# Two batches of attention products in float32, and the second layer's weight splits spread out

## The chip, the cores and the metric

The kernel runs on one core of a Trainium2 chip. The core has TensorE (PE, matrix products; PEld is its weight load), VectorE (DVE), ScalarE (ACT), GpSimd (POOL) and SyncE (SP, which only issues transfers here). The metric is the device time of one execution in microseconds (us), the median of the runs shown.

## The reference

Three steps follow each other on float32 activations and float64 weights. Shapes: 8 batches, 8 heads, 576 positions, head size 64, 32 memory slots.

```python
a = softmax over positions of phi                # per batch and head, 576 x 32
k_m, v_m = a^T k, a^T v                          # 32 x 64 each
attn = softmax(q k_m^T / 8) ; out = attn v_m     # 576 x 64
x = out as (4608, 512)
x = (silu(x @ w_gate) * (x @ w_val)) @ w_out     # 512 -> 1536 -> 512
h = x @ w_in ; g = h if h > 0 else exp(h) - 1    # 512 -> 2048
x = g @ w_out2                                   # 2048 -> 512
```

q and k are drawn 20 times as wide as the other inputs, so the scores are sharp and the products that lead to them must be close to float32.

## The kernel before, in words

**Number format.** TensorE takes float32 here in a reduced form (F32R in the code). To keep the precision, an operand is cut in two: `hi` is a copy to F32R by ACT, `lo` is the rest, subtracted by DVE or POOL. A product is then three matmuls: hi by hi, hi by lo, lo by hi. Weights come as float64 words and are cut by `split_w` (L76 to L90): ACT scales the high word (L82), DVE does four operations (L83, L84, L86, L87), ACT makes hi (L88), POOL makes lo in two operations (L89, L90). Two raw buffers (`wr`) and two pairs of work buffers (`wv`, `wc`) serve all 68 splits: 24 of `w1g` (gate and value weights), 12 of `w1o`, 32 of `w2` (16 units of the second layer with two halves each).

**Attention.** `front_tasks` of a batch transposes the softmax of phi (`a_T`), cuts five chunks of k and v (`kv_prep`), multiplies (`kv_mm`, L251), masks (`kv_out`) and transposes k_m and v_m (`k_T`, `v_T`). `back_tasks` cuts five chunks of q (`q_prep`), makes scores (`score`, L303), does the softmax over 32 slots and transposes the result into `at`. Chunk buffers come in twos, so chunk c+2 is loaded when chunk c has been cut.

**Phase 1.** For every batch, units 0 to 3 of the first layer in two halves of 288 positions: `gate1`, `val1` (its last DVE operation is `h`, L171, then `hh` by ACT and `hl` by DVE), `down1`. The attention tasks of the following batches are put between the units by `tick`. Batch 0's attention and part of batch 1's stand alone at the start.

**Phase 2.** Units 4 to 11 for every batch, 16 halves of 8 units. `vw2` and `fold` multiply attention values into the gate weights; from batch 4 on these are read back (`load_vw`, `vwl`). 16 splits of `w2` are asked for in batches 3 and 4, at every second unit; the other 16 are asked for behind the phase.

**Layer 2.** Nine blocks of 512 tokens, each 16 units: 12 matmuls up (`pu`), the ELU chain on DVE and ACT (`unit3`, L662 to L666, then `hh` and `hl`), 12 matmuls down, two units later (`LAG`).

A scheduler that builds a timeline of its own sets the order on each engine, starting from the order in which the code is written; `tc.issue_after(x)` forbids it to put what follows ahead of x. The engines then run their instructions strictly in that order.

Of the kernel before, what the change touches and what calls it, by code (L numbers as in the profile page):

```python
# [8 lines left out]
F32 = mybir.dt.float32  # L9
# [18 lines left out]
NCH = 5  # L28
NWA = 24
NWB = 22  # L30
NWD = 2
NWC = 18
NM = 4
# [3 lines left out]
def attention_moe_moe(ctx: ExitStack, tc: tile.TileContext, qT, phiT, kv, w1g, w1o, w2, out):  # L37
# [59 lines left out]
    def load_w(store, u, i, src, pool):  # L97
        raw = wr_p.tile([128, 512, 2], I32, tag="wr", name="wr")
        nc.sync.dma_start(out=raw, in_=src.rearrange("p (n t) -> p n t", t=2))
        hi = pool.tile([128, 512], F32R, tag="w", name="whi")  # L100
        lo = pool.tile([128, 512], F32R, tag="w", name="wlo")
        split_w(raw, hi, lo)
        store[u][i] = hi, lo
# [48 lines left out]

    last = {}

    def gate1(b, u, at, s0, silu):
# [11 lines left out]
    def val1(b, u, at, s0, s, silu):  # L167
        pv = ps_gv.tile([128, HS], F32, tag="g", name="pv")
        up1(pv, VW[b, u // 2], 256 * (u % 2) + 128, at, s0)
        h = t_p.tile([128, HS], F32, tag="h", name="h")  # L170
        stt(out=h, in0=s, scalar=1.0 if silu else 0.5, in1=pv, op0=ALU.mult, op1=ALU.mult)  # L171
        return split_h(h_p, h, HS)
# [19 lines left out]
    class Batch:  # L192
        def __init__(self, b):
            self.b = b
            self.kvr, self.kvs, self.qr, self.qs = {}, {}, {}, {}

        def load_phi(self):
            self.ph = fr_p.tile([128, 2, S], F32, tag="ph", name="ph")
            nc.sync.dma_start(out=self.ph, in_=phiT[self.b].rearrange("g p s -> p g s"))

        def load_kv(self, c):
            n = chunk(c)
            t = fr_p.tile([128, 2, 512], F32, tag="kvr", name="kvr", bufs=2)
            nc.sync.dma_start(out=t[:n], in_=kv[self.b, 128 * c:128 * c + n])
            self.kvr[c] = t

        def load_q(self, c):
            n = chunk(c)
            t = bk_p.tile([128, 512], F32, tag="qr", name="qr", bufs=2)
            nc.sync.dma_start(out=t[:, :4 * n], in_=qT[self.b, :, 512 * c:512 * c + 4 * n])  # L210
            self.qr[c] = t
# [387 lines left out]
    load_wf(*heads[0][:2])  # L599
    w2q = [(3, wb_p)] * 8 + [(4, wa_p)] * 8  # L600
    vwq = []
    ldq = {(2 * b - 1) * (NU1 - UA) + 2 * p - UA + 3: (b, p) for b in range(NM, B) for p in range(UA // 2, NU1 // 2)}
    for b in range(B):
        for hf in range(2):
# [4 lines left out]
            for u in range(UA, NU1):  # L609
# [44 lines left out]
    def unit3(u, xt):  # L654
# [77 lines left out]
```

## Time and profile before

| what | value |
|---|---|
| median of 3 runs (lowest, highest) | 1769.15 us (1768.7, 1770.59) |
| the profiled execution: its time, its span | 1770.36 us, 1768.6 us |
| granted TensorE clock, mean | 0.972 |
| busy share of the span: PE, DVE, ACT, POOL | 94%, 63%, 43%, 16% |
| chain that ended last: PE, DVE, DMA | 74%, 14%, 6% |

The time is 1.8 us more than the span, which runs from the first to the last instruction. A share over the whole span says little here: the four stages (start, phase 1, phase 2, layer 2) differ. The rows by stretch further down are the ones to read.

### The profile page before, as it was taken

The numbers are of one execution on the slowest core, as the hardware profiler recorded it, in microseconds if no ns is written. First come the engines' busy times: TensorE is split into PE (matmuls) and PEld (weight loads), VectorE is DVE, ScalarE is ACT, GpSimd is POOL, SyncE is SP. The second block draws the span as 40 slices with busy tenths as digits, with TensorE's granted clock in tenths as the row PEclk, the third lists the DMA queues.
The fourth block names the chain that finished last, engine by engine and source line by source line (L and its number), as shares of the span: only waits on it lengthen the run. The fifth ranks groups of instructions, "written<-read, shape, count | busy, mean of one in ns | idle before, by whom it ended". The sixth has DMA issues, their size and how long they took to land.

```text
span 1768.6 us, 24239 instructions
## 1 busy us (share of the span) xinstructions
PE 1667.3 (94%) x9296; PEld 1468.6 (83%) x9296; DVE 1108.2 (63%) x1837; ACT 760.2 (43%) x1457; POOL 282.8 (16%) x199
## 2 busy tenths in 40 slices
PE   5589999989999998889999799999999999999998
PEld 3379989979899997889998678888888888888887
DVE  7988777697853358644448965555545555555554
ACT  5456655555533344423334534343434343434332
POOL 4632222253510024200004410000000000000000
PEclk7689999999999999999999899999999999999999
DMA  6455544235624346843333301010101010101000
GB/s 218 158 196 186 169 157 157 89 135 158 208 86 157 100 128 194 252 140 106 112 102 105 109 1 48 1 48 1 48 1 48 1 48 1 48 1 48 0 24 24
DMA packets 89396, 168.57 MB, mean 95 GB/s; under 512 B 16576, under 2 KB 48320, under 8 KB 87232
## 3 DMA queue, kind: packets, MB, share of 16 engines
q1 hardware_dynamic: 65216, 132.41, 23.1%
q10 hardware_dynamic: 24064, 34.62, 6.4%
q8 instruction: 73, 1.20, 0.3%
q14 instruction: 43, 0.35, 0.1%
HBM read 108.27 MB, written 50.33 MB: 90 GB/s over the span
## 4 chain that ended last, share of the span: by engine, by line
PE 74%; DVE 14%; DMA 6%; issue 3%; ACT 2%; ACTq 0%; POOL 0%; SPq 0%; DVEq 0%; POOLq 0%
PE acc L678 7%; PE acc L677 7%; PE acc L676 7%; PE pu L651 7%; PE pu L650 7%; PE pu L652 7%; PE acc L142 3%; PE acc L143 3%; PE acc L144 3%; DVE wv L84 2%; PE pv L137 2%; PE pg L137 2%; DVE wc L87 2%; PE pv L138 2%; PE pv L139 2%
## 5 line engine op out<-in xcount | busy, mean ns | idle before, releaser
L650 PE MATMUL pu<-x1s,whi 128*128 128x512 f32 x576 | 225.0, 391 | 9.4 <-DVE g L666 9.4
L678 PE MATMUL acc<-whi,hl 128*128 128x512 f32 x576 | 222.7, 390 | 2.5 <-DVE hl L150 2.5
L676 PE MATMUL acc<-whi,hh 128*128 128x512 f32 x576 | 224.3, 389 | 0.7 <-ACT hh L148 0.7
L651 PE MATMUL pu<-x1s,whi 128*128 128x512 f32 x576 | 224.7, 390 | 0.0
L652 PE MATMUL pu<-x1s,wlo 128*128 128x512 f32 x576 | 224.6, 390 | 0.0
L677 PE MATMUL acc<-wlo,hh 128*128 128x512 f32 x576 | 224.1, 389 | 0.0
L665 DVE SCALAR_TENSOR_TENSOR g<-e,g 128x512 f32<-128x512 f32 x144 | 101.7, 707 | 162.8 <-ACT g L664 162.8
L89 POOL TENSOR_TENSOR wv<-wv,whi 128x512 f32<-128x512 f32 x68 | 103.7, 1526 | 531.9 <-ACT whi L88 434.0
L663 ACT ACTIVATE e<-g 128x512 f32<-128x512 f32 x144 | 90.6, 630 | 213.2 <-DVE g L662 213.1
L148 ACT ACTIVATE hh<-g 128x512 fp32r<-128x512 f32 x144 | 90.9, 632 | 209.2 <-DVE g L666 207.7
L171 DVE SCALAR_TENSOR_TENSOR h<-s,pv 128x288 f32<-128x288 f32 x192 | 86.0, 448 | 132.7 <-PE pv L139 115.8
L150 DVE TENSOR_TENSOR hl<-g,hh 128x512 fp32r<-128x512 f32 x144 | 100.5, 698 | 92.1 <-ACT hh L148 92.1
L142 PE MATMUL acc<-hh,whi 128*128 128x288 f32 x512 | 148.9, 295 | 5.2 <-ACT hh L148 5.2
L143 PE MATMUL acc<-hh,wlo 128*128 128x288 f32 x512 | 149.5, 295 | 0.0
L144 PE MATMUL acc<-hl,whi 128*128 128x288 f32 x512 | 143.2, 297 | 5.4 <-DVE hl L150 5.4
L150 DVE TENSOR_TENSOR hl<-h,hh 128x288 fp32r<-128x288 f32 x192 | 109.0, 570 | 61.5 <-ACT hh L148 61.1
L148 ACT ACTIVATE hh<-h 128x288 fp32r<-128x288 f32 x192 | 84.5, 442 | 139.7 <-DVE h L171 128.3
L650 PEld LDWEIGHTS pu<-x1s,whi 128*128 128x128 f32 x576 | 108.4, 188 | 32.3 <-DVE g L666 9.8
L662 DVE TENSOR_SCALAR g<-pu 128x512 f32<-128x512 f32 x144 | 99.1, 689 | 55.0 <-PE pu L652 54.9
L678 PEld LDWEIGHTS acc<-whi,hl 128*128 128x128 f32 x576 | 108.0, 188 | 26.1 <-DVE hl L150 3.7
L676 PEld LDWEIGHTS acc<-whi,hh 128*128 128x128 f32 x576 | 108.2, 188 | 23.9 <-ACT hh L148 1.5
L651 PEld LDWEIGHTS pu<-x1s,whi 128*128 128x128 f32 x576 | 108.6, 189 | 22.5
(128 smaller groups left out, 4039.0 us busy)
## 6 DMA issues: line engine op xcount, KB each, us to landing
kvr<-kv SPq DMA_DIRECT2D x32, 512.0 KB, 4.2
wr<-w SPq DMA_DIRECT2D x32, 512.0 KB, 3.6
wr<-w1g SPq DMA_DIRECT2D x24, 512.0 KB, 3.8
atd<-at SPq DMA_DIRECT2D x8, 1152.0 KB, 4.7
p1d<-p ACTq DMA_DIRECT2D x64, 144.0 KB, 2.7
at<-atd SPq DMA_DIRECT2D x8, 1152.0 KB, 7.4
p1l<-p1d SPq DMA_DIRECT2D x16, 576.0 KB, 4.5
x1d<-p1l SPq DMA_DIRECT2D x16, 576.0 KB, 3.3
```

Of the source, the lines that this page charges most:

```text
L89: nc.gpsimd.tensor_tensor(out=v, in0=v, in1=hi.bitcast(F32), op=ALU.subtract)
L142: mm(ps, lhsT=w[0][:, ms], rhs=hs[0], start=start, stop=False)
L143: mm(ps, lhsT=w[1][:, ms], rhs=hs[0], start=False, stop=False)
L144: mm(ps, lhsT=w[0][:, ms], rhs=hs[1], start=False, stop=stop)
L148: act(out=hh, in_=h, func=AF.Copy)
L150: tt(out=hl, in0=h, in1=hh.bitcast(F32), op=ALU.subtract)
L650: mm(ps, lhsT=wh[:, k, :], rhs=xh, start=k == 0, stop=False)
L651: mm(ps, lhsT=wh[:, k, :], rhs=xl, start=False, stop=False)
L652: mm(ps, lhsT=wl[:, k, :], rhs=xh, start=False, stop=k == KD - 1)
L676: mm(accs[c], lhsT=hs[0][:, cs], rhs=wh, start=u == 0, stop=False)
L677: mm(accs[c], lhsT=hs[0][:, cs], rhs=wl_, start=False, stop=False)
L678: mm(accs[c], lhsT=hs[1][:, cs], rhs=wh, start=False, stop=u == NU2 - 1)
```

## The change

Batches 0 and 1 (`NF = 2`) keep k, v, q, the softmax of phi and k_m as float32 and multiply them in one float32 matmul instead of three: no `kv_prep`, no `q_prep`, no `al`, and the scores are one matmul of 64 columns and an ACT copy instead of two matmuls, an ACT copy and a DVE addition. All five chunks of a batch are loaded in one go; they take over the buffers in which hi and lo were. `split_w` now stands behind the last `h` (or, in layer 2, the last `g`) that was written before it. The splits of `w2` are asked for one at units 5 and 9 of every half from batch 3 on (20), and two per unit in the first six units of layer 2 (12).

```diff
-NWC = 18
+NWE = 8
+NWC = 10
+NF = 2
@@ load_w
-        split_w(raw, hi, lo)
+        with tc.issue_after(last["h"].ins) if "h" in last else nullcontext():
+            split_w(raw, hi, lo)
@@ val1, and the same for the last operation of unit3
-        stt(out=h, in0=s, scalar=1.0 if silu else 0.5, in1=pv, op0=ALU.mult, op1=ALU.mult)
+        last["h"] = stt(out=h, in0=s, scalar=1.0 if silu else 0.5, in1=pv, op0=ALU.mult, op1=ALU.mult)
@@ Batch
+            self.f32 = b < NF
+            self.kv_tag = [("kvr", "kvr", "kvh", "kvh", "kvl")[c - b] if self.f32 else "kvr" for c in range(NCH)]
...
-            tt(out=self.al[o], in0=ps[:n, :nch], in1=self.ah[o].bitcast(F32), op=ALU.subtract)
+            if not self.f32:
+                tt(out=self.al[o], in0=ps[:n, :nch], in1=self.ah[o].bitcast(F32), op=ALU.subtract)
@@ kv_prep and q_prep
+            if self.f32:
+                return
@@ kv_mm
+            if self.f32:
+                t = self.kvr.pop(c)
+                for g in range(2):
+                    mm(self.kvp[g], lhsT=self.ah[:n, c, 128 * g:128 * g + 128],
+                       rhs=t[:n, :, 256 * g:256 * g + 256], start=c == 0, stop=c == 4)
+                return
@@ score
+            if self.f32:
+                q = self.qr.pop(c)[:, :4 * n].rearrange("p (i s) -> p i s", i=4)
+                ps = ps_at.tile([128, 4, 64], F32, tag="at", name="ps_sc")
+                for i in range(4):
+                    mm(ps[:n, i, :], lhsT=q[:, i, :], rhs=self.kT[:, i // 2, i % 2, 0:64], start=True, stop=True)
+                act(out=self.sc[:n, c, :], in_=ps[:n].rearrange("p i n -> p (i n)"), func=AF.Copy)
+                return
@@ the start
-    Bs[0].load_kv(0)
-    Bs[0].load_kv(1)
-    Bs[0].load_q(0)
-    Bs[0].load_q(1)
+    for c in range(NCH):
+        Bs[0].load_kv(c)
+    for c in range(NCH):
+        Bs[0].load_q(c)
@@ phase 2
-    w2q = [(3, wb_p)] * 8 + [(4, wa_p)] * 8
+    w2q = [wb_p] * 8 + [wa_p] * 8
...
-                if u % 2 == 0 and w2q and w2q[0][0] <= b:
-                    more_w2(w2q.pop(0)[1])
+                if u % 4 == 1 and b >= NM - 1:
+                    more_w2(w2q.pop(0))
+        if b == NM - 1:
+            st_vq.close()
+            we_p = ctx.enter_context(tc.tile_pool(name="we", bufs=NWE))
+            w2q += [we_p] * 4
@@ between phase 2 and layer 2
-    more_w2(wb_p, 3)
-    more_w2(wa_p, 4)
     wc_p = ctx.enter_context(tc.tile_pool(name="wc", bufs=NWC, side="right"))
-    more_w2(wc_p, len(todo2))
+    w2q = [wb_p] * 3 + [wa_p] * 4 + [wc_p] * 5
@@ layer 2, behind each unit
+            for _ in range(2):
+                if w2q:
+                    more_w2(w2q.pop(0))
```

What the scheduler makes of it is seen in three places. The first is TensorE's queue at the start, batch 0's front. Before, with `kvh` and `kvl` the cut chunks and `al` the rest of the transposed softmax:

```order
L236 MATMUL ps_aT<-ident,ph 128x128 x4
L260 MATMUL ps_kvm<-kvh,ah 128x512 x2
L236 MATMUL ps_aT<-ident,ph 128x128 x4
L261 MATMUL ps_kvm<-kvh,al 128x512
L262 MATMUL ps_kvm<-kvl,ah 128x512
L261 MATMUL ps_kvm<-kvh,al 128x512
L262 MATMUL ps_kvm<-kvl,ah 128x512
```

With the change (L244 is the transposition, L269 the float32 product, L291 the transposition of k_m):

```order
L244 MATMUL ps_aT<-ident,ph 128x128 x4
L269 MATMUL ps_kvm<-kvr,ah 128x512 x2
L244 MATMUL ps_aT<-ident,ph 128x128 x4
L269 MATMUL ps_kvm<-kvr,ah 128x512 x2
L244 MATMUL ps_aT<-ident,ph 64x128 x2
L269 MATMUL ps_kvm<-kvr,ah 128x512 x6
L291 MATMUL ps_kT<-ident,kvm 128x128 x4
```

Ten products stand where thirty stood, and nothing in the row needs a cut operand.

The second is SP's queue at the start (`ph` is phi, `kvr` and `qr` the chunks, `wr` the raw weights). Before:

```order
L199 DMA ph<-phiT 128x2x576
L204 DMA kvr<-kv 128x1024 x2
L210 DMA qr<-qT 128x512 x2
L99 DMA wr<-w1g 128x1024 x2
L204 DMA kvr<-kv 128x1024 x2
L210 DMA qr<-qT 128x512 x2
L99 DMA wr<-w1g 128x1024
L199 DMA ph<-phiT 128x2x576
```

With the change:

```order
L206 DMA ph<-phiT 128x2x576
L211 DMA kvr<-kv 128x1024 x4
L211 DMA kvr<-kv 64x1024
L217 DMA qr<-qT 128x512 x4
L217 DMA qr<-qT 128x256
L211 DMA kvr<-kv 128x1024
L103 DMA wr<-w1g 128x1024 x2
L217 DMA qr<-qT 128x512
L211 DMA kvr<-kv 128x1024 x2
```

The first two raw weights stand behind twelve loads instead of five.

The third is DVE's queue in the first units of layer 2. Before, from the first two `g` on (L83, L84, L86, L87 are the splits):

```order
L662 TENSOR_SCALAR g<-pu 128x512 x2
L83 TENSOR_SCALAR wc<-wv 128x512
L84 SCALAR_TENSOR_TENSOR wv<-wv,wc 128x512
L665 SCALAR_TENSOR_TENSOR g<-e,g 128x512 x2
L86 TENSOR_SCALAR wc<-wv 128x512
L83 TENSOR_SCALAR wc<-wv 128x512
L666 TENSOR_TENSOR g<-g,pu 128x512 x2
L87 SCALAR_TENSOR_TENSOR wc<-wr,wc 128x512
L84 SCALAR_TENSOR_TENSOR wv<-wv,wc 128x512
L150 TENSOR_TENSOR hl<-g,hh 128x512 x2
L86 TENSOR_SCALAR wc<-wv 128x512
L662 TENSOR_SCALAR g<-pu 128x512 x2
```

With the change, a few units in (L87, L88, L90, L91 are the splits, L710, L713, L714 and L155 the four operations of a unit):

```order
L90 TENSOR_SCALAR wc<-wv 128x512
L87 TENSOR_SCALAR wc<-wv 128x512
L714 TENSOR_TENSOR g<-g,pu 128x512
L710 TENSOR_SCALAR g<-pu 128x512
L91 SCALAR_TENSOR_TENSOR wc<-wr,wc 128x512
L88 SCALAR_TENSOR_TENSOR wv<-wv,wc 128x512
L155 TENSOR_TENSOR hl<-g,hh 128x512
L90 TENSOR_SCALAR wc<-wv 128x512
L713 SCALAR_TENSOR_TENSOR g<-e,g 128x512
L710 TENSOR_SCALAR g<-pu 128x512
L91 SCALAR_TENSOR_TENSOR wc<-wr,wc 128x512
L714 TENSOR_TENSOR g<-g,pu 128x512
```

The units are the same; of the splits, 14 stand from the end of phase 2 on in the row before, and 12 in the row of the change, over the first twelve units. The 16 earlier ones, which stand between the 109th and the 132nd `h` before, have become 20 between the 114th and the 190th, of 192.

## Rows read from the trace of the kernel before

**Rows 1.** busy time by stretch: start:end, length, five engines, PEclk, DMA share, GB/s
```profile
0.00:100.00 100.00, 55.81 (x184) 38.71 (x184) 87.36 (x122) 47.80 (x85) 51.38 (x41) 0.69 0.59 193
100.00:200.00 100.00, 97.20 (x651) 88.73 (x652) 84.53 (x162) 63.46 (x139) 31.36 (x19) 1.00 0.54 181
360.00:500.00 140.00, 127.11 (x821) 118.47 (x820) 122.43 (x201) 69.89 (x151) 63.97 (x47) 0.95 0.52 165
500.00:640.00 140.00, 139.70 (x961) 133.91 (x960) 49.74 (x110) 46.40 (x101) 0.00 (x0) 1.00 0.38 117
640.00:660.00 20.00, 20.00 (x138) 19.15 (x138) 13.46 (x21) 9.46 (x19) 10.44 (x8) 1.00 0.35 111
640.00:780.00 140.00, 123.14 (x806) 115.75 (x806) 91.98 (x153) 59.55 (x126) 45.47 (x32) 0.96 0.61 191
780.00:940.00 160.00, 160.00 (x1210) 160.00 (x1209) 70.78 (x155) 56.59 (x128) 0.00 (x0) 1.00 0.33 102
940.00:1030.00 90.00, 74.12 (x369) 61.91 (x369) 83.26 (x114) 42.61 (x75) 45.89 (x32) 0.94 0.31 101
1200.00:1400.00 200.00, 200.00 (x884) 165.58 (x884) 107.67 (x160) 76.51 (x123) 0.00 (x0) 1.00 0.07 22
```

**Rows 2.** DVE groups from 0 to 110: count, busy us, mean ns, idle before
```profile
L87 DVE SCALAR_TENSOR_TENSOR wc<-wr,wc 128x512 f32<-128x512 uint32 x14 | 16.4, 1168 | 0.1
L84 DVE SCALAR_TENSOR_TENSOR wv<-wv,wc 128x512 int32<-128x512 int32 x14 | 12.4, 892 | 0.1
L190 DVE TENSOR_TENSOR kvl<-kvr,kvh 128x1024 fp32r<-128x1024 f32 x7 | 11.5, 1650 | 0.7 <-ACT kvh L247 0.6
L83 DVE TENSOR_SCALAR wc<-wv 128x512 int32<-128x512 int32 x14 | 9.1, 655 | 2.9 <-ACT wv L82 2.9
L86 DVE TENSOR_SCALAR wc<-wv 128x512 int32<-128x512 int32 x14 | 6.7, 483 | 0.0
...
L190 DVE TENSOR_TENSOR ql<-qr,qh 128x512 fp32r<-128x512 f32 x4 | 3.8, 954 | 0.0
L240 DVE TENSOR_TENSOR al<-ps_aT,ah 128x512 fp32r<-128x512 f32 x5 | 3.4, 678 | 0.0
L190 DVE TENSOR_TENSOR kvl<-kvr,kvh 64x1024 fp32r<-64x1024 f32 x2 | 3.3, 1648 | 0.1
...
L315 DVE TENSOR_TENSOR sc<-ps_sc,sct 128x256 f32<-128x256 f32 x6 | 2.5, 415 | 0.1
```

**Rows 3.** DVE in order of time (start, length): the fourth h
```profile
108.42 0.45 DVE L171 SCALAR_TENSOR_TENSOR h<-s,pv 128x288 f32<-128x288 f32 x1 [0.55 <-PE pv L139]
```

**Rows 4.** TensorE in order of time: start, length, instruction
```profile
14.36 0.63 PE L261 MATMUL ps_kvm<-kvh,al 128*128 128x512 f32 x1
14.79 0.63 PE L262 MATMUL ps_kvm<-kvl,ah 128*128 128x512 f32 x1
...
36.88 0.37 PE L312 MATMUL ps_sc<-kT,ql 128*128 128x64 f32 x1
37.06 0.46 PE L311 MATMUL ps_sc<-kT,qh 128*128 128x128 f32 x1
```

**Rows 5.** waits of the whole span: who, for whom, us in total, times, longest
```profile
ACT vwl L549 <- DMA vwl<-vwd: 22.3, 14, 4.9
...
PE pu L650 <- DVE g L666: 9.4, 1, 9.4
```

**Rows 6.** DVE groups from 940 to 1025, around the start of layer 2
```profile
L665 DVE SCALAR_TENSOR_TENSOR g<-e,g 128x512 f32<-128x512 f32 x8 | 7.6, 955 | 0.0
L150 DVE TENSOR_TENSOR hl<-g,hh 128x512 fp32r<-128x512 f32 x8 | 6.4, 816 | 0.2 <-ACT hh L148 0.2
L662 DVE TENSOR_SCALAR g<-pu 128x512 f32<-128x512 f32 x9 | 5.9, 678 | 0.0
L150 DVE TENSOR_TENSOR hl<-h,hh 128x288 fp32r<-128x288 f32 x6 | 5.9, 990 | 0.5 <-ACT hh L148 0.5
...
L666 DVE TENSOR_TENSOR g<-g,pu 128x512 f32<-128x512 f32 x8 | 5.3, 676 | 0.0
```

More of the change, by code (lines that the diff above doesn't have):

```diff
@@ L1 @@
-from contextlib import ExitStack
+from contextlib import ExitStack, nullcontext
 import concourse.bass as bass
@@ L73, in attention_moe_moe @@
     x1_d = [dram.tile([128, KD, S], F32, name=f"x1d{b}") for b in range(B)]
+    last = {}
     def split_w(raw, hi, lo):
@@ L151, in split_h @@
         return hh, hl
-    last = {}
     def gate1(b, u, at, s0, silu):
@@ L195, in __init__ @@
             self.kvr, self.kvs, self.qr, self.qs = {}, {}, {}, {}
+            self.f32 = b < NF
+            self.kv_tag = [("kvr", "kvr", "kvh", "kvh", "kvl")[c - b] if self.f32 else "kvr" for c in range(NCH)]
+            self.q_tag = [("qr", "qr", "qh", "qh", "ql")[c - b] if self.f32 else "qr" for c in range(NCH)]
         def load_phi(self):
@@ L202, in load_kv @@
             n = chunk(c)
-            t = fr_p.tile([128, 2, 512], F32, tag="kvr", name="kvr", bufs=2)
+            t = fr_p.tile([128, 2, 512], F32, tag=self.kv_tag[c], name="kvr", bufs=2)
             nc.sync.dma_start(out=t[:n], in_=kv[self.b, 128 * c:128 * c + n])
@@ L208, in load_q @@
             n = chunk(c)
-            t = bk_p.tile([128, 512], F32, tag="qr", name="qr", bufs=2)
+            t = bk_p.tile([128, 512], F32, tag=self.q_tag[c], name="qr", bufs=2)
             nc.sync.dma_start(out=t[:, :4 * n], in_=qT[self.b, :, 512 * c:512 * c + 4 * n])
@@ L227, in a_T @@
             if c0 == 0:
-                self.ah = fr_p.tile([128, NCH, 256], F32R, tag="ah", name="ah")
-                self.al = fr_p.tile([128, NCH, 256], F32R, tag="al", name="al")
+                self.ah = fr_p.tile([128, NCH, 256], F32 if self.f32 else F32R, tag="ah", name="ah")
+                if not self.f32:
+                    self.al = fr_p.tile([128, NCH, 256], F32R, tag="al", name="al")
             n = min(128, S - 128 * c0)
@@ L239, in a_T @@
             act(out=self.ah[o], in_=ps[:n, :nch], func=AF.Copy)
-            tt(out=self.al[o], in0=ps[:n, :nch], in1=self.ah[o].bitcast(F32), op=ALU.subtract)
+            if not self.f32:
+                tt(out=self.al[o], in0=ps[:n, :nch], in1=self.ah[o].bitcast(F32), op=ALU.subtract)
         def kv_prep(self, c):
+            if self.f32:
+                return
             n = chunk(c)
@@ L275, in k_T @@
                                     in_=self.kvm[:, i // 2, 0, 128 * (i % 2):128 * (i % 2) + 128], identity=ident)
-            self.kT = bk_p.tile([128, 2, 2, 128], F32R, tag="kT", name="kT")
+            self.kT = bk_p.tile([128, 2, 2, 128], F32 if self.f32 else F32R, tag="kT", name="kT")
             for r in range(2):
+                if self.f32:
+                    act(out=self.kT[:, :, r, 0:64], in_=ps[:, :, r, 64 * r:64 * r + 64], func=AF.Copy)
+                    continue
                 p, hi = ps[:, :, r, 64 * r:64 * r + 64], self.kT[:, :, r, 0:64]
@@ L294, in q_prep @@
         def q_prep(self, c):
+            if self.f32:
+                return
             n = 4 * chunk(c)
@@ L306, in score @@
                 self.sc = bk_p.tile([128, NCH, 256], F32, tag="sc", name="sc")
+            if self.f32:
+                q = self.qr.pop(c)[:, :4 * n].rearrange("p (i s) -> p i s", i=4)
[3 more added lines that the diff above has]
+                act(out=self.sc[:n, c, :], in_=ps[:n].rearrange("p i n -> p (i n)"), func=AF.Copy)
+                return
             qh, ql = (a[:, :4 * n].rearrange("p (i s) -> p i s", i=4) for a in self.qs.pop(c))
@@ L357, in front_tasks @@
         z, nxt = Bs[b], Bs[b + 1] if b + 1 < B else None
+        if b < NF:
+            yield lambda: (z.a_T(0), z.kv_mm(0))
+            yield lambda: (z.a_T(2), z.kv_mm(1))
+            yield lambda: (z.a_T(4), z.kv_mm(2), z.kv_mm(3), nxt.load_phi())
+            yield lambda: (z.kv_mm(4), z.kv_out(), [nxt.load_kv(c) for c in range(NCH if nxt.f32 else 2)])
+            yield lambda: (z.k_T(), z.v_T())
+            return
         yield lambda: (z.a_T(0), z.kv_prep(0), z.load_kv(2))
@@ L367, in back_tasks @@
         z, nxt = Bs[b], Bs[b + 1] if b + 1 < B else None
+        if b < NF:
+            yield lambda: (z.score(0), z.score(1))
+            yield lambda: (z.score(2), z.soft(0, 2))
+            yield lambda: (z.score(3), z.score(4))
+            yield lambda: (z.soft(2, 4), z.soft(4, 5), [nxt.load_q(c) for c in range(NCH if nxt.f32 else 2)],
+                           b and Bs[b + 2].phi())
+            yield lambda: (z.soft2(0, 2), z.attn_T(0, 2), setattr(z, 'mark1', z.mark))
+            yield lambda: (z.soft2(2, 4), z.soft2(4, 5), z.attn_T(2, 5), z.store_at())
+            return
         yield lambda: (z.q_prep(0), z.load_q(2))
@@ L491, in attention_moe_moe @@
     wd_p = st_p1.enter_context(tc.tile_pool(name="wd", bufs=NWD, side="right"))
-    vq_p = st_p1.enter_context(tc.tile_pool(name="vq", bufs=1, side="right"))
-    wf_p = st_p1.enter_context(tc.tile_pool(name="wf", bufs=2, side="right"))
+    st_vq = ExitStack()
+    vq_p = st_vq.enter_context(tc.tile_pool(name="vq", bufs=1))
+    wf_p = st_vq.enter_context(tc.tile_pool(name="wf", bufs=2))
     load_wo(7, wa_p)
@@ L665, in unit3 @@
         stt(out=g, in0=e, scalar=1.0, in1=g, op0=ALU.add, op1=ALU.mult)
-        tt(out=g, in0=g, in1=p, op=ALU.max)
+        last["h"] = tt(out=g, in0=g, in1=p, op=ALU.max)
         return split_h(h3_p, g, T)
```

## The prediction

> **What bounds the kernel now.** I read the windows by stretch first, since a share over the whole span mixes four stages. In each row the reader is to set TensorE's busy time against the length of the stretch, then look at the granted clock, then at DVE. Where TensorE is full the stretch can't get shorter without less work on it: 500 to 640, 780 to 940 and 1200 to 1400, where 884 matmuls of 512 columns take 200 us, 0.226 each [rows 1]. Where it is not full, what it loses is the idle time plus the part of its busy time that the clock (mean below 1.00, so partly at 1.2 instead of 2.4 GHz) wastes: 44.2 + 0.31 x 55.8 = 61.5 us from 0 to 100; 12.9 + 0.05 x 127.1 = 19.3 from 360 to 500; 16.9 + 0.04 x 123.1 = 21.8 from 640 to 780; 15.9 + 0.06 x 74.1 = 20.3 from 940 to 1030 [rows 1]. These are 123 us of loss, and all four stretches are those with weight splits in them: POOL, which after phase 1 does nothing but splits, is busy in them and at 0.00 in the full ones, and DVE stands at 66% to 93% against 36% to 54% [rows 1]. Second view: the DVE groups of the start, for what it does there [rows 2]. Third: the waits, of which one names the edge of layer 2 outright, PE 9.4 us for a `g` of DVE [rows 5]. So in the lossy stretches DVE is the bound, and behind it POOL.
>
> **The change part by part.**
>
> *Start.* Before the fourth `h` of batch 0 (108.4 us) [rows 3] DVE does the lo parts of batches 0 and 1 and 14 splits. It loses: `kvl` 11.5 + 3.3, less one that is batch 2's (1.65), so 13.2; `ql` 3.8; `al` 3.4 less one of batch 2 (0.68), so 2.7; the score additions 2.5: together 22.2 [rows 2]. A split costs it (16.4 + 12.4 + 9.1 + 6.7) / 14 = 3.2 [rows 2]; by the new order 11 instead of 14 stand ahead of the fourth `h`, 9.6 less. That is 31.8 off a queue that idles 12.6 of its first 100 us [rows 1]. POOL also gives up its share of batch 1's lo parts; where it works, L87 and L84 take 1168 and 892 ns against 678 for a `g` that reads as many columns from PSUM [rows 2, 6], an excess of 14 x (0.49 + 0.21) = 9.8, of which I take half back, 5.
>
> What is late next: the products themselves. A float32 matmul is nowhere in the trace. From below it is one reduced matmul, 0.226 at the higher clock; from above I take the dearest column in the rows, 0.18 us for 64 columns at the lower clock (36.88 to 37.06), so 1.44 for 512 [rows 1, 4]. I take 1.28, what the three it replaces cost at that clock (14.36 to 14.79, three times 0.43) [rows 4], which is near the upper end and makes the work on TensorE equal to before. Batch 0's ten then run from about 10 us, when the softmax of phi has been transposed, to about 23, and only then has DVE more than two splits to do. The raw weights are behind twelve loads on SP, but nothing is late by that: the first two splits are needed after these products. DVE so idles about 10 us longer than before. Batch 1's ten products go into time in which TensorE still waits. Score matmuls: one for two, 64 columns for 192, taken as equal. Sum: -31.8 - 5 + 10 = -27. The three splits put off (9.6) fall into 100 to 200, where DVE has 15.5 us free [rows 1]: hidden; if that cover is gone, they cost up to 9.6. Ends: -42 if a product costs 0.226 and DVE never waits for it; -10 if it costs 1.44, batch 1's are in the way too (10 x 1.44) and POOL's relief fails.
>
> By the Trainium skill (FP8 and Floating Point Precision, TensorE Precision Notes) true float32 takes four passes through the array; no run here shows it so far. Four times the two prices of the reduced matmul would be 0.90 and 1.72, an estimate that makes twenty products some 4.5 us dearer than the sixty they replace at the higher clock, and the forecast would be 1719 by it.
>
> *Phase 2.* From 640 to 780 DVE is busy 42.2 us more than from 500 to 640 [rows 1]; with 16 splits that is 2.6 each. With them gone from there and 20 spread over the 300 us from 640 to 940, DVE has 92.0 - 42.2 + 70.8 + 20 x 2.6 = 173 us, 58%, and no longer bounds anything. What stays is the way of the last fold through memory into batch 4, `vwl` (waits of 4.9 at most, 22.3 in all) [rows 5]; I leave 7 us for that, and 1 for the later splits. 21.8 - 8 = 14 gained; ends 5 (the loss is all `vwl` and DMA) and 20.
>
> *Edge of layer 2.* A unit costs TensorE 24 x 0.226 = 5.43 us, DVE 107.7 / 884 x 24 = 2.9 when alone [rows 1]. The new order puts 12 splits among the first twelve units, one each: 2.9 + 2.6 = 5.5, level with TensorE. By the longer times beside POOL, 0.96 + 0.82 + 0.68 + 0.68 + 3.2 = 6.3 [rows 2, 6], it would be 0.9 too much per unit, 11 us. Between 1 and 11 I take 6, since the order leaves DVE no backlog at the edge. 20.3 - 6 = 14 gained; ends 9 and 19. The wait of 9.4 goes; late next is `g` behind a split, by fractions of a microsecond.
>
> *360 to 500.* The same 24 splits, begun behind the 48th `h` instead of the 43rd: 0, ends -6 and +8.
>
> Sum against the profiled execution: 1770.4 - 27 - 14 - 14 = 1715.4; it lies 1.2 above the median, so 1714. All upper ends together give 1682, all lower ones 1756.
>
> **The rivals.**
>
> *The products take the place of the cuts* (17%). TensorE then bounds the start, at the lower clock, and only 5 us of the 27 remain: 1714 + 22 = 1736. For it: the clock of 0.69 from 0 to 100 [rows 1] and that no row prices a float32 product. Against: TensorE was idle 44 us there.
>
> *The start gains its upper end* (15%): products near 0.226 or well hidden, 15 more, 1699. For it: POOL's part in DVE's times [rows 2]; against: raw weights that come later.
>
> *Slower: POOL beside a full TensorE* (5%). The splits now stand in stretches that were full, and each has two POOL operations, 45.47 / 32 = 1.42 us apiece [rows 1]. If every one held up an `hl` for its whole length and TensorE with it, 64 x 1.42 = 91 us against 55 gained: 1805. It decides from 55 / 64 = 0.86 us per operation on. For it: `hl` of 288 columns takes 990 ns around 940, longer than a `g` of 512 [rows 6]. Against: from 640 to 660 POOL is busy 10.4 of 20 and TensorE 20.00 of 20 [rows 1], so single splits beside it cost nothing. The Trainium skill (SBUF — State Buffer, SBUF: two separate sides) says that GpSimd and a DVE operation with two SBUF inputs hold their shared ports exclusively, so that "the other fully blocks". By that rule each such meeting costs DVE time; the 990 ns agree. It has 5%, for one row that speaks for it and one against.
>
> *It does nothing* (3%): the scheduler trades every gain for a wait elsewhere; 1769.
>
> **How the numbers follow.** The forecast, 1714 with its own range 1702 to 1728, has 60%. Eight times in ten the time should lie between 1694 and 1742: this takes in the first two rivals and leaves out the slower one, no change, and the ends of the terms that would all have to fall together. Measurements tell 0.2%, 3.5 us, from no change. Faster: 60 + 17 + 15 = 92%; the same 3%; slower 5%.
>
> **What would show it.** Right: the fourth `h` at about 81 us; TensorE idle under 10 us in the 140 us that answer to 640 to 780, and DVE there near 58%; no wait of `pu` for `g` over 3 us at the edge; POOL active in single splits through phase 2. Wrong: float32 products over 1.5 us each with DVE waiting for `kvm` past 30 us; splits on DVE that wait for raw weights or for a free buffer while an `h` stands behind them; TensorE less than full between batch 4 and the end of phase 2.

## The result, and the profile after

The changed kernel takes 1722.85 us (median of 4 runs, 1721.68 to 1725.53), the kernel before 1769.41 (4 runs, 1768.70 to 1770.59): a ratio of 0.9738, 95% interval 0.9721 to 0.9755, so 46.6 us less where 55 were forecast. The profiled span went from 1768.6 to 1719.9, 48.7 less.

First view, stretches of the changed kernel, to be read beside [rows 1] (start:end, length, PE, PEld, DVE, ACT, POOL busy with counts, granted clock, DMA share, GB/s). The work of 640 to 780 now lies some 26 us earlier, that of the edge (940 to 1030) near 890 to 1000.

```profile
0.00:100.00 100.00, 75.46 (x320) 51.04 (x320) 81.63 (x127) 51.26 (x105) 47.07 (x39) 0.89 0.67 230
20.00:100.00 80.00, 63.28 (x291) 45.61 (x290) 77.72 (x120) 44.87 (x94) 45.12 (x27) 0.86 0.61 203
300.00:500.00 200.00, 186.51 (x1242) 171.35 (x1241) 166.15 (x280) 96.88 (x214) 78.89 (x57) 0.99 0.44 143
613.00:753.00 140.00, 132.09 (x913) 125.66 (x912) 66.55 (x132) 52.79 (x115) 20.59 (x14) 1.00 0.54 168
740.00:890.00 150.00, 149.06 (x1116) 147.78 (x1115) 98.83 (x189) 62.91 (x140) 37.93 (x24) 1.00 0.47 147
890.00:1000.00 110.00, 103.42 (x545) 88.10 (x544) 92.33 (x139) 52.16 (x92) 43.49 (x29) 1.00 0.27 87
1150.00:1350.00 200.00, 200.00 (x884) 165.58 (x883) 108.10 (x160) 75.87 (x122) 0.00 (x0) 1.00 0.07 22
```

In 140 us of phase 2 TensorE idles 7.9 us instead of 16.9, POOL is down from 45.47 to 20.59, and the next 150 us, which hold 12 splits now, are still full (149.06). The edge loses 6.6 in 110 where it lost 20.3 in 90. In the first 100 us TensorE still idles 24.5, and DVE is busy 81.63, of which 77.72 lie in the 80 us from 20 on: there it is still the bound.

Second view, the timeline, worked out from the traces: when the n-th `h` of phases 1 and 2 ends (192 in all), and the span. The gain is before less after; the columns behind it belong to the experiments.

```
 h      before   after  gain |   e1     e2     e7     e4     e5
   1     103.3    66.9  36.4 |  68.1  104.6   67.2   77.4   61.1
   4     108.9    91.8  17.1 |  93.6  110.1   92.6   99.5   88.6
  16     194.1   168.4  25.7 | 173.4  195.3  173.5  171.8  164.1
  48     389.7   352.1  37.6 | 365.6  391.1  364.8  355.9  344.6
  72     501.5   475.8  25.7 | 479.5  500.7  478.9  466.1  451.3
 108     644.3   618.2  26.1 | 621.6  644.7  620.1  614.3  601.1
 138     783.3   743.0  40.3 | 757.2  769.2  757.9  737.3  725.8
 174     897.9   861.2  36.7 | 871.6  889.7  870.5  855.5  844.0
 span   1768.6  1719.9  48.7 | 1742.2 1748.8 1733.2 1704.9 1693.0
```

So 26 us come from the start; `h` 48 is 12 more ahead, which is gone again by `h` 72; phase 2 brings 14.2, of which 3.6 are given back up to `h` 174; the edge brings the last 12.0. Up to the sixteenth `h` (194.07 before, 168.42 after), DVE's busy time fell by 33.2 us, and its idle time grew by 7.5, from 27.9 to 35.4:

```profile
0.00:194.07 194.07, 147.08 (x793) 121.78 (x794) 166.15 (x272) 107.05 (x214) 81.99 (x58) 0.84 0.56 188
0.00:168.42 168.42, 143.33 (x775) 114.08 (x776) 133.00 (x234) 92.39 (x195) 67.03 (x51) 0.92 0.63 211
```

Third view, single rows of the start: TensorE (start, length, instruction), then ACT and DVE.

```profile
9.18 3.50 PE L269 MATMUL ps_kvm<-kvr,ah 128*128 128x512 f32 x4 [0.69 <-ACT ah L247]
14.88 5.51 PE L269 MATMUL ps_kvm<-kvr,ah 128*128 128x512 f32 x12
```

```profile
16.92 0.67 ACT L86 ACTIVATE wv<-wr 128x512 f32<-128x512 f32 x1 [1.46 <-DMA wr<-w1g]
17.62 0.43 DVE L87 TENSOR_SCALAR wc<-wv 128x512 int32<-128x512 int32 x1 [9.68 <-ACT wv L86]
19.66 0.75 DVE L285 SCALAR_TENSOR_TENSOR kvm<-ps_kvm,rs,mask 128x512 f32<-128x512 f32 x1
91.40 0.44 DVE L174 SCALAR_TENSOR_TENSOR h<-s,pv 128x288 f32<-128x288 f32 x1
```

And the groups of the products up to 100 us:

```profile
L269 PE MATMUL ps_kvm<-kvr,ah 128*128 128x512 f32 x32 | 18.9, 732 | 2.2 <-ACT ah L247 2.2
L269 PE MATMUL ps_kvm<-kvr,ah 64*128 64x512 f32 x8 | 4.0, 615 | 0.0
```

A float32 product appears as two records (40 for the 20 products). Six take 5.51 us, 0.92 each; this holds the length of the last record and a pause, and from start to start a product takes 0.86. The first two take 3.33 to the next instruction, 1.67 each. The ten of batch 0 run from 9.18 to 20.39, 1.1 on average. DVE idles 9.7 us for its first split, and that wait is for the raw weights: ACT, on which DVE waits, has itself waited for `wr`. The first split begins at 17.62, two microseconds before `kvm`. The fourth `h` [rows 3] is at 91.40.

Fourth view, DVE's groups from 890 to 1000, against [rows 6] (count, busy, mean ns, idle before).

```profile
L91 DVE SCALAR_TENSOR_TENSOR wc<-wr,wc 128x512 f32<-128x512 uint32 x14 | 17.4, 1250 | 0.1
L713 DVE SCALAR_TENSOR_TENSOR g<-e,g 128x512 f32<-128x512 f32 x12 | 11.4, 952 | 0.3 <-ACT g L712 0.3
L155 DVE TENSOR_TENSOR hl<-g,hh 128x512 fp32r<-128x512 f32 x12 | 10.7, 895 | 0.8 <-ACT hh L153 0.8
L87 DVE TENSOR_SCALAR wc<-wv 128x512 int32<-128x512 int32 x14 | 10.3, 745 | 0.0
L710 DVE TENSOR_SCALAR g<-pu 128x512 f32<-128x512 f32 x13 | 8.9, 683 | 1.4 <-PE pu L700 1.3
L714 DVE TENSOR_TENSOR g<-g,pu 128x512 f32<-128x512 f32 x12 | 8.2, 679 | 0.1
```

The two groups that read `pu` from PSUM keep their 0.68; those with all inputs in SBUF are long (what they take without POOL is seen in e4). Fifth view, TensorE's waits there (who, for whom, us, times, longest): the 9.4 us for `g` [rows 5] is gone, small waits for `hl` and `hh` are left.

```profile
PE acc L726 <- DVE hl L155: 4.1, 5, 1.8
PE acc L724 <- ACT hh L153: 2.5, 3, 1.1
```

Two pairs of rows show why such an operation is long. DVE first, POOL second:

```profile
954.56 1.46 DVE L91 SCALAR_TENSOR_TENSOR wc<-wr,wc 128x512 f32<-128x512 uint32 x1
959.64 1.78 DVE L91 SCALAR_TENSOR_TENSOR wc<-wr,wc 128x512 f32<-128x512 uint32 x1
```

```profile
954.18 1.29 POOL L93 TENSOR_TENSOR wv<-wv,whi 128x512 f32<-128x512 f32 x1 [2.23 <-DVE wc L90]
959.40 1.47 POOL L93 TENSOR_TENSOR wv<-wv,whi 128x512 f32<-128x512 f32 x1 [1.90 <-ACT whi L92]
```

The DVE operation that starts inside a POOL operation ends about 0.55 us behind POOL's end (956.02 behind 955.47, 961.42 behind 960.87), as if it had begun its work only there.

### The profile page after: what moved, and what is told of

The parts are those of the page before. It is cut to its first block, busy times and chain, and to the rows that moved or that the text cites. A ratio compares the mean times of both kernels' runs of the same rounds, so it can differ in the third digit from the quotient of the medians.

```text
span 1719.9 us, 24095 instructions
## 1 busy us (share of the span) xinstructions
PE 1657.2 (96%) x9276; PEld 1451.1 (84%) x9276; DVE 1074.1 (62%) x1804; ACT 742.9 (43%) x1437; POOL 278.4 (16%) x192
## 4 chain that ended last, share of the span: by engine, by line
PE 74%; DVE 11%; DMA 5%; issue 2%; ACT 1%; ACTq 0%; DVEq 0%; SPq 0%
PE acc L725 7%; PE acc L724 7%; PE acc L726 7%; PE pu L700 7%; PE pu L699 7%; PE pu L698 7%; PE acc L147 3%; PE acc L149 3%; PE acc L148 3%; PE pg L142 2%; PE pv L142 2%; PE pv L143 2%; PE pg L143 2%; PE pv L144 2%; PE pg L144 2%; DVE wc L91 2%
## 5 line engine op out<-in xcount | busy, mean ns | idle before, releaser
L713 DVE SCALAR_TENSOR_TENSOR g<-e,g 128x512 f32<-128x512 f32 x144 | 102.8, 714 | 158.1 <-ACT g L712 158.1
L93 POOL TENSOR_TENSOR wv<-wv,whi 128x512 f32<-128x512 f32 x68 | 110.4, 1624 | 508.4 <-DVE wc L90 410.9
L155 DVE TENSOR_TENSOR hl<-g,hh 128x512 fp32r<-128x512 f32 x144 | 102.0, 709 | 88.9 <-ACT hh L153 88.8
L155 DVE TENSOR_TENSOR hl<-h,hh 128x288 fp32r<-128x288 f32 x192 | 114.4, 600 | 58.1 <-ACT hh L153 57.9
L710 DVE TENSOR_SCALAR g<-pu 128x512 f32<-128x512 f32 x144 | 99.3, 690 | 54.5 <-PE pu L700 54.4
L725 PEld LDWEIGHTS acc<-wlo,hh 128*128 128x128 f32 x576 | 108.2, 188 | 22.6
L698 PEld LDWEIGHTS pu<-x1s,whi 128*128 128x128 f32 x576 | 108.2, 188 | 22.5
```

The lines of the kernel that those rows point to most:

```text
L93: nc.gpsimd.tensor_tensor(out=v, in0=v, in1=hi.bitcast(F32), op=ALU.subtract)
L155: tt(out=hl, in0=h, in1=hh.bitcast(F32), op=ALU.subtract)
L698: mm(ps, lhsT=wh[:, k, :], rhs=xh, start=k == 0, stop=False)
L725: mm(accs[c], lhsT=hs[0][:, cs], rhs=wl_, start=False, stop=False)
```

## The experiments

Theory A: the gain is DVE's work, taken off the start (26) and spread in phase 2 and at the edge. The cuts of code are shortened. Rivals: the float32 products are the start's new bound; the parts lean on each other; POOL beside DVE is what matters. Every kernel was timed beside the kernel before on its own chip; ratios are against that, with 95% intervals.

**e1, e2: the two halves apart.**

```diff
 e1: as after, but
-            we_p ... w2q += [we_p] * 4        (splits of layer 2 as before)
-        with tc.issue_after(last["h"].ins) ...
 e2: as after, but
-NF = 2
+NF = 0        (two chunks loaded first; edge behind h for layer 2's splits alone)
```

> The kernel before, with the float32 products and the early loads of batches 0 and 1 alone; the splits of layer 2's weights stand where they stood. My theory (the start is DVE's, and the two parts of the change add up): 26 us less than before, 1743, all of it gained before the twentieth h; from 500 us on nothing changes. Rival (the start gains because splits are held behind an h, and the products bring little): less than 10 us, 1760 or more.

> The kernel before, with the new places of layer 2's splits alone (attention products cut as before, splits of phase 1 not held behind an h). My theory: phase 2 gains 11 and the edge of layer 2 gains 10, so 21 to 22 less than before, 1748, and e1 and e2 together give the whole gain of 46.5. Rival (the parts lean on each other: the new places are worth something only behind a shorter start, or cost in the stretch from 360 to 500): the two gains miss 46.5 by more than 6.

Measured: e1 1744.47 (ratio 0.9866, 0.9835 to 0.9897), e2 1749.97 (0.9885, 0.9865 to 0.9905), before in that call 1771.11: 26.6 and 21.1 less. Together 47.7, against 46.6 measured for both. The halves add up. In the table e1 has 23 of its gain by `h` 108 and 26 by `h` 138, so "nothing changes" from 500 us on misses by some 4; e2 has none by then, 14.1 by `h` 138 and loses 5.9 again to `h` 174. That all of it would be gained before the twentieth `h` was too sharp: 20.7 were there.

**e3: batch 2 in float32 too** (`NF = 3`).

> The changed kernel with batch 2's products in float32 too. My theory (DVE bounds the first 100 us still, and batch 2's lo parts, kvl 7.6 and al 1.8 us, lie in them): 5 to 9 less than the changed kernel, 1714 to 1718. Rival (TensorE is now the bound of the start, the ten products cost it 10 x 0.9 for 30 x 0.23): 2 to 4 more, 1725 to 1727.

Measured: 1717.62 (0.9701, 0.9686 to 0.9716), 5.2 less than after. The products cost TensorE more (0.86 to 0.92 against 3 x 0.226), and the kernel is faster: DVE was still the bound.

**e4: POOL's part of a split on DVE.**

```diff
-        nc.gpsimd.tensor_tensor(out=v, in0=v, in1=hi.bitcast(F32), op=ALU.subtract)
-        nc.gpsimd.tensor_tensor(out=lo, in0=v, in1=cf, op=ALU.add)
+        tt(out=v, in0=v, in1=hi.bitcast(F32), op=ALU.subtract)
+        tt(out=lo, in0=v, in1=cf, op=ALU.add)
```

> The changed kernel with the two last operations of every weight split on DVE instead of POOL: 2 x 68 operations of 512 columns, 0.68 each, 92 us more work for DVE. My theory (a POOL operation holds up a DVE operation whose inputs both lie in SBUF until it ends: at the edge of layer 2 that makes DVE 19.9 us longer over 28 POOL operations, 0.71 each, so DVE loses as much by waiting as by doing it itself): within 5 us of the changed kernel, 1718 to 1728, and hl, wc and e,g operations fall back to 0.68. Rival (the long DVE operations come from something else, such as DMA): DVE is the bound in some 250 us with 122 of these operations, 0.68 each, so 40 to 80 us more, 1763 or later.

Measured: 1703.85 (0.9623, 0.9604 to 0.9641), 19.0 less than after; both expectations missed in time, the rival's by 60 on the other side; that `hl`, `wc` and `g<-e,g` fall back to 0.69 was right. DVE got 136 operations more and is busy less. The first part of the page, after and then e4:

```profile
PE 1657.2 (96%) x9276; PEld 1451.1 (84%) x9276; DVE 1074.1 (62%) x1804; ACT 742.9 (43%) x1437; POOL 278.4 (16%) x192
```

```profile
PE 1654.4 (97%) x9276; PEld 1457.1 (85%) x9276; DVE 1057.9 (62%) x1940; ACT 739.3 (43%) x1437; POOL 70.5 (4%) x56
```

DVE's groups of e4 from 884 to 994, and the stretch at the edge:

```profile
L155 DVE TENSOR_TENSOR hl<-g,hh 128x512 fp32r<-128x512 f32 x14 | 9.6, 688 | 0.8 <-ACT hh L153 0.8
L91 DVE SCALAR_TENSOR_TENSOR wc<-wr,wc 128x512 f32<-128x512 uint32 x14 | 9.6, 687 | 0.0
L713 DVE SCALAR_TENSOR_TENSOR g<-e,g 128x512 f32<-128x512 f32 x15 | 10.3, 687 | 0.0
L87 DVE TENSOR_SCALAR wc<-wv 128x512 int32<-128x512 int32 x14 | 5.8, 423 | 0.0
```

```profile
890.00:1000.00 110.00, 110.00 (x566) 95.39 (x565) 96.30 (x180) 55.28 (x99) 0.00 (x0) 1.00 0.26 86
```

Against these, after's edge lost (1250 - 687) x 14 + (745 - 423) x 14 + (952 - 687) x 12 + (895 - 688) x 12 ns, 18.1 us of DVE, over 29 POOL operations. In e4 DVE is busier there (96.30 against 92.33) and TensorE is full. By the table e4 is 3.4 behind at `h` 16, 3.9 ahead at `h` 108, 5.7 at `h` 174 and 15.0 at the end (the profiled execution of e4 is the slowest of its four, 1706.67): 7 gained between `h` 16 and 108, 9 at the edge. The scheduler's order changed with the engine (10 splits stand ahead of the first `h` where 8 stood); what part of the 19 that makes was not tested.

**e5: the two together**, `NF = 3`, POOL for a split only ahead of the first `h`.

```diff
+        eng = nc.vector if "h" in last else nc.gpsimd
+        eng.tensor_tensor(out=v, ...)        (both operations)
```

> Batch 2's products in float32 too, and the two last operations of a split on DVE from the first h on, on POOL before it. My theory (POOL helps where DVE is the bound and nothing else waits for it, up to about 90 us, where e4 fell 3.4 us behind; behind that its operations only hold DVE up, and e4 gained 8 in 360 to 500 and 9 at the edge): the gains of e3 (5) and e4 (19) and those 3.4 add up, 1694 to 1699. Rival (e4's gain hangs on the start too, or batch 2's float32 products now stand on a TensorE that is the bound): no better than e4, 1702 to 1706.

Measured: 1694.38 (0.9563, 0.9537 to 0.9589), as expected. Up to the first `h` POOL seems to help: e4 has it 10.5 later than after, and e5 at 61.1, as e3 does (61.6), which keeps POOL throughout.

**e6: the products twice.**

```diff
+                    for r in range(2):
                         mm(self.kvp[g], lhsT=self.ah[...], rhs=t[...], ...)
```

> The changed kernel with each of the 20 float32 products of kvm issued twice into the same sum (kvm comes out doubled). One product took 0.86 at the higher clock and 1.66 to 1.79 at the lower, the ten of a batch 11.3 and 10.4 us. My theory (DVE bounds the start; it has two to four splits to do while batch 0's products run, and batch 1's run while TensorE waits anyway): half of 21.7 at most shows, 5 to 11 more than the changed kernel, 1728 to 1734. Rival (the products have taken the place of the cuts as the bound of the start): all of it shows, 1743 or more.

Measured: 1731.31 (0.9777, 0.9755 to 0.9800), 8.5 more than after, inside theory A's range. So the products aren't wholly hidden, and aren't the whole bound: 8.5 of 21.7 shows. `kvm` moved from 19.66 to 28.95. The 8.5 is no clean price: the scheduler put 12 splits ahead of the first `h` where 8 stood, the first `h` ends at 87.0 instead of 66.9 and the sixteenth at 181.5 instead of 168.4, so 13.1 are lost at first and part of it comes back.

**e7: without the edge behind `h`.**

```diff
-        with tc.issue_after(last["h"].ins) if "h" in last else nullcontext():
+        with nullcontext():
```

> The changed kernel without the edge that holds each split behind the last h issued before it (phase 1, phase 2 and layer 2). My theory (the places of the splits in the program's order do the work, the edge adds little; e1 without it kept the start's gain): within 4 us of the changed kernel, 1719 to 1727. Rival (without it splits move ahead of the h again, in 360 to 500, phase 2 and at the edge): 10 to 20 us more.

Measured: 1737.59 (0.9810, 0.9788 to 0.9832), 14.7 more; the rival was right. The stretch that answers to [rows 1]'s 640 to 780, and the next:

```profile
613.00:753.00 140.00, 126.30 (x824) 117.56 (x824) 102.60 (x167) 64.74 (x135) 56.59 (x40) 0.96 0.64 199
740.00:890.00 150.00, 147.38 (x1089) 146.34 (x1090) 78.82 (x158) 55.32 (x125) 8.98 (x6) 0.98 0.39 121
```

40 POOL operations instead of 14 lie in the first, 6 instead of 24 in the second: the scheduler moved the splits forward again. At `h` 108 the kernel is 1.9 behind after, at `h` 138 14.9: the 13.0 in between are nearly all of phase 2's gain (14.2).

**e8, e11: a POOL operation beside a full TensorE.** Both have all splits on DVE, as e4.

```diff
 e8, per unit of blocks 2 to 9:
+    for _ in range(2):
+        nc.gpsimd.tensor_tensor(out=dead[0], in0=dead[1], in1=dead[2], op=ALU.subtract)
 e11, per unit of blocks 2 to 9:
+    nc.gpsimd.tensor_tensor(out=dead, in0=hs3[1].bitcast(F32), in1=hs3[1].bitcast(F32), op=ALU.subtract)
```

> All splits wholly on DVE as in e4, and two dead POOL subtractions of 512 columns (SBUF to SBUF) in each of the 128 units of blocks 2 to 9 of layer 2, where TensorE is full: it prices a POOL operation beside a full TensorE. My theory (each holds up one DVE operation on SBUF alone by about 0.7 us; DVE stands at 54% there and has the room): DVE busy 150 to 200 us longer, hl and e,g groups near 1.0 instead of 0.70, and the time within 10 us of e4, 1702 to 1714. Rival (the slower rival of the prediction: every operation holds an hl and TensorE with it for 1.42): 256 x 1.42 = 364 us more; half of that where only every second one meets an hl.

> All splits wholly on DVE as in e4, and one dead POOL subtraction of 512 columns per unit in blocks 2 to 9 of layer 2, which reads that unit's hl, so that it can't run ahead as the 256 of e8 did (there POOL ran without a break from 912 to 1320 us). Price of single POOL operations beside a full TensorE. My theory (DVE stands at 54%, and a unit has two units' time until its hl is needed; a single hold of up to 1.4 us fits into that): DVE busy longer by 40 to 100 us over 128 of them, the time within 5 us of e4, 1700 to 1709. Rival (each costs what e8's cost on average, 125.7 / 256 = 0.49): 63 more, 1767.

Measured: e8 1829.52 (1.0333, 1.0309 to 1.0357), 125.7 more than e4; e11 1703.47 (0.9622, 0.9599 to 0.9646), the same as e4. In e8 nothing held the dead operations, so POOL ran them without a break, from 922 to 1328 us: it tests a POOL that never pauses, not two per unit. Theory and rival both missed. Its stretches and DVE groups of 1150 to 1350 (POOL ends at 1328):

```profile
900.00:1000.00 100.00, 73.60 (x310) 59.23 (x308) 91.69 (x86) 29.00 (x49) 75.66 (x51) 0.85 0.14 46
1000.00:1100.00 100.00, 67.22 (x221) 50.32 (x220) 96.93 (x78) 24.52 (x41) 95.14 (x63) 0.80 0.09 29
1100.00:1200.00 100.00, 92.04 (x380) 70.85 (x378) 70.43 (x71) 32.30 (x53) 94.98 (x65) 0.98 0.07 22
```

```profile
L156 DVE TENSOR_TENSOR hl<-g,hh 128x512 fp32r<-128x512 f32 x33 | 47.7, 1446 | 22.2 <-ACT hh L154 22.0
L714 DVE SCALAR_TENSOR_TENSOR g<-e,g 128x512 f32<-128x512 f32 x32 | 35.9, 1123 | 37.3 <-ACT g L713 37.2
L711 DVE TENSOR_SCALAR g<-pu 128x512 f32<-128x512 f32 x33 | 22.4, 679 | 0.0
```

With splits on DVE as well (900 to 1100) DVE stands at 92 and 97%, and TensorE idles 26 and 33 of 100, at a lower clock besides; without them, DVE at 70%, it still idles 8. In e11, with one POOL operation per unit that starts behind `hl`, DVE's `g<-e,g` stands at 713 (692 in after) and TensorE is full:

```profile
1150.00:1350.00 200.00, 200.00 (x884) 165.62 (x883) 108.55 (x159) 75.99 (x123) 38.39 (x37) 1.00 0.07 22
L745 POOL TENSOR_TENSOR dead<-hl 128x512 f32<-128x512 f32 x37 | 39.1, 1058 | 162.1 <-DVE hl L155 162.1
```

But e11 tests less than it was made for. Beside 93 of its 128 POOL operations only DVE operations that read PSUM start (nearly always `g<-pu`, which keeps its length), beside 25 none, and beside 10 one with all inputs in SBUF. Two of them, POOL first:

```profile
1159.32 1.04 POOL L745 TENSOR_TENSOR dead<-hl 128x512 f32<-128x512 f32 x1 [4.40 <-DVE hl L155]
1159.63 0.69 DVE L710 TENSOR_SCALAR g<-pu 128x512 f32<-128x512 f32 x1 [0.45 <-PE pu L700]
1189.21 1.36 POOL L745 TENSOR_TENSOR dead<-hl 128x512 f32<-128x512 f32 x1 [5.35 <-DVE hl L155]
1189.94 1.18 DVE L713 SCALAR_TENSOR_TENSOR g<-e,g 128x512 f32<-128x512 f32 x1 [0.27 <-ACT g L712]
```

So it shows that a POOL operation that meets PSUM readers costs nothing. What a hold in every unit would cost TensorE stays open.

**e9: the lo parts put back as dead work.**

```diff
+                if self.b == 0 or not LO_KV[c]:
+                    tt(out=dead, in0=t, in1=t, op=ALU.subtract)        (and for q of batch 0)
```

> The changed kernel with dead DVE subtractions in the size of the lo parts that left it (kv and q of batch 0: 5 x 1.2 + 4 x 0.68 + 0.41 = 9.1 us; kv of batch 1, three pieces, 3.6 us), whose results nothing reads and on which no product waits. It asks whether every microsecond off DVE counted, as the prediction's sum took it. My theory now (in the changed kernel DVE idles 9.7 us up to 17.6 for the first raw weights, and batch 0's lo parts fit into that hole; only batch 1's count): 3 to 5 more than the changed kernel, 1726 to 1728. Rival (the prediction's sum: all of it counts): 12.7 more, 1735.5.

Measured: 1730.46 (0.9773, 0.9758 to 0.9788), 7.6 more: between the two, neither right. Batch 0's ten operations do fit into the hole; the first split begins at 17.46 against 17.62:

```profile
12.84 3.33 DVE L338 TENSOR_TENSOR dead<-qr 128x512 fp32r<-128x512 f32 x5
17.46 0.43 DVE L87 TENSOR_SCALAR wc<-wv 128x512 int32<-128x512 int32 x1 [1.28 <-ACT wv L86]
```

What is left is 7.6 us for batch 1's 3.6, twice their length. The scheduler also placed the first `h` later (87.1 instead of 66.9); how much is that and how much is DVE stays open.

**e10, e12: e5 improved.** e10 loads the first two raw weights ahead of batch 0's q (and `phi()` is called ahead of both); e12 puts the other batches' lo parts on DVE too.

```diff
 e10:
+    load_wg(0, 0, wa_p)
+    load_wg(0, 1, wa_p)
     for c in range(NCH):
         Bs[0].load_q(c)
 e12:
-        eng = nc.gpsimd if pool_engine else nc.vector
+        eng = nc.vector
```

> The kernel of e5 (1694.4) with the first two raw weights loaded ahead of batch 0's q chunks instead of behind them. q is 1.15 MB, 2.8 us at the 419 GB/s of the first 17 us. My theory (DVE waits for the first raw weights until 17.3, and is the bound from there to the first h): the first split begins 2 to 3 us earlier and the kernel ends 2 to 3 us earlier, 1691 to 1693. Rival (the scores, which now get q later, or kvm at 19.6, set the pace of the start): no change within 1.5, or later.

> The kernel of e5 with the lo parts of kv and q of batches 3 to 7 on DVE as well; POOL then does splits before the first h and nothing behind it. In e5 POOL's 28 operations from 100 to 300 us lengthen DVE's by 16.4 us and take 46.6 themselves. My theory (moved, they cost DVE about what the holds cost it, and TensorE loses only 4.6 there): within 3 us of e5, 1691 to 1697. Rival (as with the splits, the holds fall on hl and cost TensorE more than DVE's time shows): 4 to 8 less, 1686 to 1690.

Measured: e10 1687.36 (0.9531, 0.9515 to 0.9546), 7.0 less than e5 where 2 to 3 were expected; the intervals of the two ratios just touch, their runs do not (1685.98 to 1689.38 against 1691.02 to 1694.86). The mean over the first 17 us of e5 is 332 GB/s (419 is the rate of single slices), by which q takes 3.5. The first split begins at 13.28 instead of 17.33; up to `h` 16 that is worth the expected 2.3 (161.8 against 164.1), the rest comes behind it and wasn't traced to a cause. e12 1690.44 (0.9549, 0.9524 to 0.9573): its runs, 1686.69 to 1695.42, lie on both sides of e5's, so nothing follows.

## Why the prediction was right, and where it missed

The time lies in the range (1694 to 1742) and in the likeliest case's own (1702 to 1728); the mechanism, DVE as the bound of the stretches with splits, is what DVE's rows and e3 show (less work for DVE, dearer products, a faster kernel); e1 and e2 show that the two parts add up. Of the 55 us, 48.7 came in the profiled executions; each term:

- *Start*, -27: -26. Right in size, in part for wrong reasons. DVE's hole was there (9.7), but for the raw weights and not for the products: "nothing is late by that" was the step that failed, and e10 shows the load order was worth something. The -31.8 counted all lo parts, while batch 0's lie in that hole (e9). Up to the sixteenth `h`, the terms -36.8 of work and +10 of idling came out as -33.2 and +7.5, so two errors offset each other, which is luck. The fourth `h` came at 91.8, not 81, because softmax and lo parts of the next batches now stand ahead of it; the sixteenth has the 25.7. The lower end, -10, does not follow from what it names: -31.8 + 10 + 14.4 is -7.4, or -5.8 with ten products at 1.44 in the hole; nor does 1756, since the lower ends add up to 1753.
- *Product price*, 1.28: 1.1 on average, 0.86 to 0.92 and 1.67 at its two speeds. The Trainium skill (FP8 and Floating Point Precision, TensorE Precision Notes) says that true float32 takes four passes. The trace agrees: 0.86 and 0.92 are 3.8 and 4.1 times the 0.226 of [rows 1], and 1.67 is 3.9 times the 0.43 of [rows 4]. By its estimate, 0.90 and 1.72, the forecast would have been 1719, nearer than mine. The first rival (1736) is refuted by e3, with e6 on the same side, the upper end of the start (1699) by the 26.
- *Phase 2*, -14: -14.2 up to `h` 138, as forecast, and TensorE's idle is under 10 as named (7.9). The mis-sized term is the "1 for the later splits": 3.6 were given back. DVE stood at 48%, not 58%, since fewer splits lay in that stretch. What makes nearly all of the gain is the edge that holds a split behind an `h` (e7, 13.0), which the sum took for granted as a new order.
- *Edge*, -14: -12.0. TensorE idles 6.6, as I took (6); no `g` is waited for.
- *360 to 500*, 0: 0 at `h` 72, with 12 lent in between.
- *The profile against the median*: 1.2 below for after, 1.2 above for before: 2.4 of the 8.9 by which the forecast missed.

The slower rival, POOL beside a full TensorE, did not decide, but its mechanism is real and I gave too little to it: in the changed kernel POOL's part of the splits cost 9 us at the edge and 7 between `h` 16 and `h` 108, against having it on DVE (e4). By the Trainium skill (SBUF — State Buffer, SBUF: two separate sides) a DVE operation with two SBUF inputs, or in a two-port mode, and a GpSimd operation that reads SBUF lock each other out of a shared port pair. The trace agrees: `hl` 895 against 688 and `wc` 745 against 423 beside POOL, and no change where an input is in PSUM (679 and 683). The price depends on what DVE does beside POOL: 1.42 for each would have been 91 us; single operations that meet mostly PSUM readers cost nothing (e11), an unbroken row of them 126 us (e8).

## What to carry to other kernels

Before work is put on POOL to relieve DVE, compare the mean lengths of DVE's groups with and without POOL beside them, PSUM readers apart from the rest: here the relief cost DVE more time than it saved (1074.1 against 1057.9), and taking it back was worth 19 us. A new place for work in the source is only worth something if the scheduler is held to it. When work leaves an engine at the start, look which load its next instruction waits for: here two loads moved forward were worth 2.3 us up to `h` 16, and 7.0 in all.

## What was not expected of the hardware

- A held DVE operation ends behind POOL's end by nearly its own length: 0.55 us for those of 512 columns with two inputs in SBUF (the pairs above; 0.69 without POOL), 0.28 for the `TENSOR_SCALAR` of a split (0.42 without):

```profile
967.65 1.51 DVE L87 TENSOR_SCALAR wc<-wv 128x512 int32<-128x512 int32 x1
967.26 1.62 POOL L94 TENSOR_TENSOR wlo<-wv,wc 128x512 fp32r<-128x512 f32 x1
```

- POOL's operations grow too: 1.26 to 1.30 us where no DVE operation on SBUF alone runs beside (11 operations of the splits in the kernel before, 2 in the changed one; the first row is one), 1.51 to 1.56 at the edge. The 1.06 of e11 is for an operation that reads one tile twice. POOL's spans are rough in the profile.

```profile
733.20 1.28 POOL L89 TENSOR_TENSOR wv<-wv,whi 128x512 f32<-128x512 f32 x1 [15.03 <-ACT whi L88]
L94 POOL TENSOR_TENSOR wlo<-wv,wc 128x512 fp32r<-128x512 f32 x15 | 23.4, 1562 | 6.9 <-DVE wc L91 6.4
L93 POOL TENSOR_TENSOR wv<-wv,whi 128x512 f32<-128x512 f32 x14 | 21.1, 1508 | 57.3 <-DVE wc L90 53.5 <-ACT whi L92 3.8
```

- The granted clock is given as 1.00 from 9 to 12.5 us, the upper level, while the first two float32 products run at half the later speed (1.67 against 0.86). In the kernel before the reduced matmuls at 14.36 to 14.79 show the same, 0.43 apart [rows 4] and not 0.226. Batch 1's first products, from 40.7 to 45.8, start as far apart (0.85 from record to record), and there the column says 0.50. So in the first microseconds, up to 12.5 in the one kernel and 17.3 in the other, the pitch tells the speed and the clock column doesn't.

```profile
9.00:12.50 3.50, 3.32 (x4) 1.41 (x5) 0.00 (x0) 0.12 (x1) 0.00 (x0) 1.00 1.03 277
40.70:45.80 5.10, 5.10 (x9) 2.51 (x10) 5.10 (x11) 2.24 (x6) 2.27 (x2) 0.50 0.04 5
```
